# A linear-attention and mixture kernel on one core: the place of w_k's first half in the load queue, and a planner bias of 60000 or 20000

## The chip, the core and the metric

The kernel runs on one core of a Trainium2 chip. The metric is the device time of one execution in microseconds (us); less is better. The times shown are single executions of one program and their median.

## The reference

Inputs come as float64 or float32 arrays; the outputs are float32. Three stages follow one another:

- Linear attention on x (4 batches, 8 heads, 768 positions, 32 wide) with decay a and the projections B and C (16 wide), in chunks of 32 with a carried state: within a chunk `M = (C B^T) * exp(cum_i - cum_j)`, causal, and `y = M x`; across chunks `y += C state * exp(cum)`, and the state is decayed and updated by `B^T x`.
- A gated feed-forward on the 3072 tokens (256 wide): `xk` and `xr` mix each token with the one before it (`mu_k`, `mu_r`); `k = relu(xk w_k)` with w_k 256 x 1024, `v = k*k w_v`, `r = sigmoid(xr w_r)`, result `r * v`.
- A maxout layer: `h = max(x w1, x w2, x w3)` (768 wide), result `h w_out` (256 wide).

## The kernel before

**Tiles.** Tokens are worked on in six tiles of 512 (`t` = 0 to 5), features lie on the 128 partitions. For each tile the kernel computes attention, `gate` (mix, w_r, tanh), `ffn` (mix, w_k, square, w_v), `combine`, `maxout` and `final`. Every product is made of three fp32r products, high by high, high by low and low by high, so each operand exists as two tiles: a rounded copy (suffix h) and the remainder (suffix l). The remainder is made by `sub` (L421), which runs on VectorE (DVE) or GpSimd (POOL).

**Weights.** They arrive as float64 and are turned into the two fp32r tiles by `load_split` (L616): one load; one ACT instruction (L630); four DVE instructions on the bit patterns (L631, L633, L635, L637); one rounded copy (`copy`, L411, on ACT or DVE; the trace gives its line as L414 or L416); one `sub` (L422). For w_k's first half, the columns 0 to 511, this is done in two pieces of 128 rows, called w_k0 and w_k1 here (loop L659 to L661); each is 512 KB. The feed-forward of tile 0 needs both pieces in its first product group, w_k0 before w_k1 (L1006).

**The order of the work** is not written out: `Plan` (L76) collects every operation with its cost, its dependencies and a bias. `forward` (L138) simulates the five engines and SyncE's load queue (SP), and takes for each engine the ready operation with the smallest key minus bias. The key is minus the time from the operation to the end of the plan, in ns. It is re-estimated by `backward` in up to 60 rounds, and the round with the shortest modelled span is issued. A bias of 20000 thus lets an operation go ahead of work that is due up to 20 us sooner.

```
heapq.heappush(ready[e], (key[i] - ops[i][4] + (spare if len(costs) > 1 and e == "DVE" else 0.0), i))   # L191
plan.bias = AHEAD[1]                                                             # L656
..., 1, FF // 2, [b_wk[c][0]], FIRST[4] - 1.5e5 * c, place=spots[c])             # L661
```

The first loads are put in order by large values of FIRST that are added to the bias of the load alone (`dma`, L425). Before the change they stand as follows: a_l (`la`, 112 KB) 1.04e6, the mus 1.035e6 (2 KB), C padded with zeros (`cw`, 512 KB), B (`bt`, 256 KB) and w_k0 all 1.01e6, `bl` (256 KB) 1.005e6, w_r (512 KB) 1.003e6, x (`xt`, 512 KB) 1.0e6, C (`ct`, 256 KB) 0.98e6, w_k1 (512 KB) 0.86e6. All are issued from SP (L427). The loads of w_k's second half and of tile 1 depend on the operation at L848 (`ce`) (`after=k`, L663).

**The front of the kernel.** `attention(0)` (L793) spreads the decays (`spread_first`, L694: PE L703 and L704, ACT L708 into `lt`), forms the scores C B^T from bt and cw in two parts (`cb`, L860), multiplies them by the decays on DVE (L872, eight instructions), sums the values (L895), adds the carried part (L885) and copies the result to `xb` (L933). Then `mix` (L958) makes the inputs of `gate(None, 0)` (products L986) and of `ffn(None, 0)` (products L1011). Biases of the operations: attention(0) and w_r's preparation 20000, the tail of attention(0) 30000 less, gate 80000, w_k0 and w_k1 and the mix of ffn(0) 60000 (AHEAD). Until the first product of a gate the plan fills gaps of PE with dummy products (L1169, issued in L324 to L326). After that it does not.

Of the kernel before, what the change touches and what calls it, by code (L numbers as in the profile page):

```python
# [75 lines left out]
class Plan:  # L76
# [14 lines left out]
    FIRST = 1500.0  # L91
# [17 lines left out]
    def op(self, eng, cost, fn, r=(), w=(), after=(), issue=475.0, unless=None, hold=None, burst=0, lock=False):  # L109
        deps = set(after)  # L110
        for b in r:
            deps.update(b.writers)
        for b in w:
            deps.update(b.readers)
            deps.update(b.writers)
        i = len(self.ops)
        costs = eng if isinstance(eng, dict) else {eng: cost}
        self.ops.append((costs, fn, sorted(deps), issue, self.bias, unless, hold or {}, burst, lock))
        for b in w:
            b.writers = [i]  # L120
            b.readers = []
        for b in r:
            b.readers.append(i)
        return i
# [212 lines left out]
SPREAD = 2  # L337
LATE = 0
EARLY1 = -20000.0
AHEAD = (60000.0, 60000.0)  # L340
FIRST = (9.85e5, 9.8e5, 9.9e5, 9.83e5, 9.5e5, 9.95e5, 9.6e5)


# [1 line left out]
def kernel(  # L345
# [24 lines left out]
    FF = w_k.shape[1]  # L370
# [54 lines left out]
    def dma(cost, out_, in_, r=(), w=(), first=0.0, **k):  # L425
        plan.bias += first
        i = op("SP", 0.8 * cost, lambda: Q.dma_start(ap(out_), in_), r=r, w=w, **k)  # L427
        plan.bias -= first
        return i
# [15 lines left out]
    b_wk = [[Buf(), Buf()] for _ in range(KC)]  # L445
# [170 lines left out]
    def load_split(src, hi, lo, k, n, bufs, early=0.0, small=False, after=(), place=None):  # L616
        m = k * n
        if place:
            (sv, ss), (wv, ws) = place
        elif small:  # L620
            s, (wv, ws) = outr.next(), word2.next(m)
            sv, ss = s.ap[:, :2 * m], [s]
        else:
            (sv, ss), (wv, ws) = stage.next(2 * m), word.next(m)
        raw = sv.bitcast(U32).rearrange("p (k n s) -> p k n s", k=k, s=2)
        high, low = raw[:, :, :, 1], raw[:, :, :, 0]
        lf = wv.rearrange("p (k n) -> p k n", k=k)
        lu = lf.bitcast(U32)
        first = dma(m * 3.65, raw.rearrange("p k n s -> p k (n s)"), src.bitcast(U32), w=ss, first=early, after=after)
        op("ACT", act(m), lambda: A.activation(lf, high.bitcast(F32), AF.Abs), r=ss, w=ws)  # L630
        op("DVE", 68 + 0.521 * m, lambda: V.tensor_scalar(  # L631
            out=lf, in0=lf, scalar1=F64_LO, scalar2=F64_HI, op0=ALU.max, op1=ALU.min), w=ws, lock=True)
        op("DVE", 68 + 0.521 * m, lambda: V.tensor_scalar(  # L633
            out=lu, in0=lu, scalar1=5, scalar2=2, op0=ALU.logical_shift_left, op1=ALU.logical_shift_right), w=ws, lock=True)
        op("DVE", tt(m), lambda: V.scalar_tensor_tensor(  # L635
            out=lu, in0=high, scalar=0xC0000000, in1=lu, op0=ALU.bitwise_and, op1=ALU.bitwise_or), r=ss, w=ws, lock=True)
        op("DVE", tt(m), lambda: V.scalar_tensor_tensor(  # L637
            out=lu, in0=low, scalar=29, in1=lu, op0=ALU.logical_shift_right, op1=ALU.bitwise_or), r=ss, w=ws, lock=True)
        copy(hi, lf, m, ws, bufs)
        sub(lo, lf, hi, m, ws + bufs, bufs)  # L640
        return first
# [3 lines left out]
    def weights_front():  # L645
        plan.bias = BIAS[2]
        dma(100, mu.rearrange("p i c -> p (i c)"), mus, w=[b_mu], first=FIRST[5])
        op("DVE", 100, lambda: V.tensor_scalar(
            out=om, in0=mu, scalar1=-1.0, scalar2=1.0, op0=ALU.mult, op1=ALU.add), r=[b_mu], w=[b_om])
        fs = [slice(0, FF // 2), slice(FF // 2, FF)]  # L650
        wide, narrow = [Buf(), Buf()], [Buf(), Buf()]
        b_pre.extend(wide[:1] + narrow[:1])
        plan.bias = BIAS[1]
        load_split(w_r.rearrange("p (k n) -> p k n", k=KC), wr_t[0], wr_t[1], KC, CH, [b_wr], FIRST[3],
                   place=(stage.next(2 * TW), word.next(TW)))
        plan.bias = AHEAD[1]  # L656
        spots = [(stage.next(2 * TW), word.next(TW)), ((wo_f[0][:, :2 * TW], wide[:1]), word.next(TW)),
                 (stage.next(4 * TW), (wo_f[1][:, :2 * TW], narrow[:1]))]
        for c in range(KC):  # L659
            load_split(w_k[c * P:(c + 1) * P, None, fs[0]], wk_t[0][:, c:c + 1, fs[0]], wk_t[1][:, c:c + 1, fs[0]],  # L660
                       1, FF // 2, [b_wk[c][0]], FIRST[4] - 1.5e5 * c, place=spots[c])  # L661
        plan.bias = 0.0
        k = [begun['loads']]  # L663
        load_split(w_k[:, fs[1]].rearrange("(c p) n -> p c n", p=P), wk_t[0][:, :, fs[1]], wk_t[1][:, :, fs[1]],
                       KC, FF // 2, [b_wk[c][1] for c in range(KC)], FIRST[4] - 4e5, place=spots[2], after=k)
        inputs(1, (FIRST[4] - 4.2e5, FIRST[4] - 4.3e5), after=k)
        dma(935, bt.rearrange("p u i -> p (u i)"), b_t[1], w=[b_bt], first=FIRST[4] - 4.4e5, after=k)
        dma(1870, cw.rearrange("p u i -> p (u i)"), c_w[1], w=[b_cw], first=FIRST[4] - 4.5e5, after=k)
        dma(935, ct.rearrange("p u i -> p (u i)"), c_t[1], w=[b_ct], first=FIRST[4] - 2e5)
        for f in range(FC // 4):  # L670
            load_split(w_v[f].rearrange("p (k n) -> p k n", k=4), wv_t[0][:, 4 * f:4 * f + 4], wv_t[1][:, 4 * f:4 * f + 4], 4, CH, [b_wv[f]])
# [89 lines left out]
    def inputs(t, early=(0.0, 0.0), after=()):  # L761
        dma(935, bl.rearrange("p g n -> p (g n)"), b_l[t], w=[b_bl], first=early[0], after=after)
        dma(1870, xts[t % 2].rearrange("p g d -> p (g d)"), x_l[t], w=[b_xt[t % 2]], first=early[1], after=after)
        op({"DVE": tt(512), "POOL": pool(512)}, 0, lambda e: (V if e == "DVE" else G).tensor_mul(
            bd, bl, dfj[:, t * NG:(t + 1) * NG, None].to_broadcast([P, NG, N])), r=[b_bl, b_df], w=[b_bd], lock=True)
# [192 lines left out]
    def mix(i, dst, bufs, half, t):  # L958
        hv, cols, bs, n = tokens(half)
        xb, b_xb = xbs[t % 2], b_xbs[t % 2]  # L960
        for c in range(KC):
            tm = tmp.next()
            tv = tm.ap[:, :n].rearrange("p (b s) -> p b s", s=P)
            op({"DVE": 129 + 0.521 * n, "ACT": 93 + act(n)}, 0, lambda e, tv=tv, c=c: (
                V.tensor_scalar_mul(tv, xb[:, c, bs, 1:], mu[:, i, c:c + 1]) if e == "DVE" else
                A.activation(tv, xb[:, c, bs, 1:], AF.Copy, scale=mu[:, i, c:c + 1])),
               r=b_xb[bs] + [b_mu], w=[tm], lock=True)
            op("DVE", 61 + tt(n), lambda tv=tv, c=c: V.scalar_tensor_tensor(  # L968
                out=tv, in0=xb[:, c, bs, :P], scalar=om[:, i, c:c + 1], in1=tv, op0=ALU.mult, op1=ALU.add),
               r=b_xb[bs] + [b_om], w=[tm], lock=True)  # L970
            split(tm.ap[:, :n], tm, [d[:, cols] for d in dst[c]], [[bufs[c][s][h] for h in hv] for s in range(2)], n)
# [23 lines left out]
    def ffn(half, t):  # L995
        hv, cols, bs, n = tokens(half)
        xkt, b_xkt = xk_hl[t % 2], b_xk[t % 2]
        plan.bias += AHEAD[0] * (t == 0)
        mix(0, xkt, b_xkt, half, t)
        plan.bias -= AHEAD[0] * (t == 0)  # L1000

# [125 lines left out]
    plan.switch = begun['spread'], begun['carried']  # L1127
    plan.bias = 0.0
    weights_front()
    sums()  # L1130
    weights_back()
# [93 lines left out]
```

## Time and profile before

| | before |
|---|---|
| median of three runs | 407.53 us (407.53 to 408.23) |
| the profiled execution | 408.05 us |
| its span in the profile | 406.3 us |
| PE busy | 396.3 us, 98% of the span |
| DVE busy | 257.9 us, 63% |
| ACT busy | 216.1 us, 53% |
| POOL busy | 55.0 us, 14% |
| granted TensorE clock, mean | 0.998 |
| moved by DMA | 31.55 MB |

The span runs from the first to the last instruction of the profile; the execution's own time is 1.75 us longer. PE is TensorE's matmuls, PEld its weight loads, SPq the load queue of SyncE. A busy share over the whole span is a mean over stages with different limits: DVE has 63% of the span but is nearly full in its first third. In a row of the timeline the numbers are start and duration in us, then engine, line, operation, output and inputs; the bracket gives the idle time of that engine before it and what ended it.

### The profile page before, as it was taken

Reading aid. Unit: us, or ns where it says so; the run is one execution under the profiler, and the core shown is the slowest. Engines: PE = TensorE matmul, PEld = TensorE weight load, DVE = VectorE, ACT = ScalarE, POOL = GpSimd, SP = SyncE. Lnnn points to the kernel's source line nnn. Section 1 sums busy time; section 2 is a strip of 40 time slices with the busy share of each in tenths; the row PEclk is TensorE's granted clock in tenths of the full one; section 3 lists DMA queues with packets and bytes.
Section 4 is the critical chain, followed back from the end, with each engine's and each line's share of the span. In section 5 each row is a group of like instructions: output and inputs, shape, how many; then the busy total and the mean of one; then the engine's idle time right before and its main releaser. Section 6 shows DMA issues by size and latency. Waiting matters only on the chain.

```text
span 406.3 us, 8667 instructions
## 1 busy us (share of the span) xinstructions
PE 396.3 (98%) x3684; PEld 318.0 (78%) x3684; DVE 257.9 (63%) x417; ACT 216.1 (53%) x379; POOL 55.0 (14%) x60
## 2 busy tenths in 40 slices
PE   8789999999999999999999999999999999999996
PEld 5557877788877888888888888888787888888885
DVE  5898999999998945573735473755373315430632
ACT  6489878954767743355743255753246733321321
POOL 5121000000004100421400231320022200010010
PEclk9999999999999999999999999999999999999999
DMA  7596559541335200206100002300000000001001
GB/s 251 187 369 193 180 139 259 164 141 33 129 112 152 73 26 0 71 38 177 31 27 0 28 2 66 66 26 0 2 2 27 0 26 2 0 0 54 0 2 52
DMA packets 12879, 31.55 MB, mean 78 GB/s; under 512 B 1768, under 2 KB 4136, under 8 KB 12072
## 3 DMA queue, kind: packets, MB, share of 16 engines
q1 hardware_dynamic: 12840, 30.99, 24.7%
q8 instruction: 29, 0.48, 0.5%
q14 instruction: 10, 0.08, 0.1%
HBM read 27.64 MB, written 3.34 MB: 76 GB/s over the span
## 4 chain that ended last, share of the span: by engine, by line
PE 80%; DVE 13%; issue 2%; DMA 2%; ACT 2%; SPq 0%; DVEq 0%; ACTq 0%
PE pa L689 32%; PE pa L1032 14%; PE pa L1011 13%; PE pa L1108 9%; PE pa L986 3%; PE pb L1108 2%; DVE L L872 2%; DVE tmp L1070 1%; PE pb L895 1%; DMA h<-in_w_k_dram 1%; PE pb L860 1%; DVE k2l L422 1%; DMA outs<-in_w_out_dram 1%; DVE tmp L968 1%; DVE h L637 1%
## 5 line engine op out<-in xcount | busy, mean ns | idle before, releaser
L1070 DVE TENSOR_TENSOR tmp<-tmp,pa 128x512 f32<-128x512 f32 x72 | 49.0, 684 | 55.3 <-PE pa L689 54.5
L422 DVE TENSOR_TENSOR k2l<-tmp,k2h 128x512 fp32r<-128x512 f32 x53 | 39.9, 764 | 40.9 <-ACT tmp L1020 34.0
L414 ACT ACTIVATE hr<-tmp 128x512 fp32r<-128x512 f32 x35 | 22.1, 632 | 69.3 <-DVE tmp L1070 69.1
L1032 PE MATMUL pa<-k2h,wvh 128*128 128x512 f32 x96 | 38.2, 398 | 0.0
L1032 PE MATMUL pa<-k2h,wvl 128*128 128x512 f32 x96 | 38.0, 395 | 0.0
L1032 PE MATMUL pa<-k2l,wvh 128*128 128x512 f32 x96 | 37.8, 393 | 0.0
L1108 PE MATMUL pa<-hr,worh 128*128 128x512 f32 x120 | 37.4, 393 | 0.0
L1017 ACT ACTIVATE tmp<-pa 128x512 f32<-128x512 f32 x48 | 28.3, 590 | 10.3 <-PE pa L1011 8.6
L1068 ACT ACTIVATE tmp<-pa 128x512 f32<-128x512 f32 x36 | 21.5, 598 | 21.8 <-PE pa L689 20.2
L1018 ACT ACTIVATE k2h<-tmp 128x512 fp32r<-128x512 f32 x48 | 30.2, 631 | 2.6 <-PE pa L1032 1.0
L422 DVE TENSOR_TENSOR hr<-tmp,hr 128x512 fp32r<-128x512 f32 x28 | 19.5, 700 | 14.8 <-ACT hr L414 14.7
L1108 PEld LDWEIGHTS pa<-hr,worh 128*128 128x128 f32 x120 | 22.3, 188 | 5.3 <-ACT th L991 0.7
L422 POOL TENSOR_TENSOR hr<-tmp,hr 128x512 fp32r<-128x512 f32 x8 | 10.3, 1292 | 110.8 <-ACT hr L414 110.8
L1020 ACT ACTIVATE tmp<-tmp 128x512 f32<-128x512 f32 x37 | 23.2, 630 | 0.8
L1108 PE MATMUL pa<-hr,worl 128*128 128x512 f32 x60 | 23.4, 389 | 0.0
L1032 PEld LDWEIGHTS pa<-k2h,wvh 128*128 128x128 f32 x96 | 18.0, 188 | 4.4 <-ACT k2h L414 0.2
L1032 PEld LDWEIGHTS pa<-k2h,wvl 128*128 128x128 f32 x96 | 18.0, 188 | 4.4
L1032 PEld LDWEIGHTS pa<-k2l,wvh 128*128 128x128 f32 x96 | 18.0, 188 | 4.1
L790 POOL TENSOR_TENSOR sbd<-sbd,um 128x256 f32<-128x256 f32 x2 | 3.1, 1548 | 117.8 <-DVE sbd L788 117.8
L1079 ACT ACTIVATE outs<-pa 128x512 f32<-128x512 f32 x9 | 5.4, 600 | 25.5 <-PE pa L1108 25.5
L968 DVE SCALAR_TENSOR_TENSOR tmp<-xb,bits,tmp 128x512 f32<-128x512 f32 x24 | 17.2, 745 | 0.3
L872 DVE TENSOR_TENSOR L<-pb,L 128x512 f32<-128x512 f32 (+1 forms) x28 | 15.7, 603 | 1.6 <-PE pb L860 0.8
(273 smaller groups left out, 977.4 us busy)
## 6 DMA issues: line engine op xcount, KB each, us to landing
h<-in_w_dram SPq DMA_DIRECT2D x6, 768.0 KB, 5.0
L<-crd SPq DMA_DIRECT2D x8, 512.0 KB, 6.9
cw<-in_c_w_dram SPq DMA_DIRECT2D x6, 512.0 KB, 4.5
xt<-in_x_l_dram SPq DMA_DIRECT2D x6, 512.0 KB, 7.8
out_dram<-outs SPq DMA_DIRECT2D x10, 256.0 KB, 2.0
h<-in_w_v_dram SPq DMA_DIRECT2D x2, 1024.0 KB, 7.6
bt<-in_b_t_dram SPq DMA_DIRECT2D x6, 256.0 KB, 4.7
bl<-in_b_l_dram SPq DMA_DIRECT2D x6, 256.0 KB, 6.5
```

What stands on the lines that cost most here:

```text
L414: A.activation(ap(out_), ap(in_), AF.Copy)
L422: op({"DVE": tt(n), "POOL": pool(n, narrow)}, 0, lambda e: (V if e == "DVE" else G).tensor_sub(ap(out_), ap(x0), ap(x1)), r=r, w=w, after= ...
L689: T.matmul(pt, l, r_, start=(i == 0), stop=(i == last))
L872: op("DVE", tt(2 * step * HP), lambda q=q, b=b, lq=lq: V.tensor_mul(lq, W[q].ap[:, b * P:(b + step) * P].rearrange("p (b r i) -> p r b i", ...
L1011: T.matmul(p.ap[:, :n], l, r_, start=(c == 0 and i == 0), stop=(c == KC - 1 and i == 2))
L1017: op("ACT", 51 + 0.833 * n, lambda: A.activation(sq, p.ap[:, :n], AF.Relu), r=[p], w=[tm])
L1018: op("ACT", act(n), lambda: A.activation(hi, sq, AF.Square), r=[tm], w=[kb])
L1020: A.activation(sq, sq, AF.Square) if e == "ACT" else
L1032: T.matmul(pv[c2].ap[:, :n], l, r_, start=(f == 0 and i == 0), stop=(f == FC - 1 and i == 2))
L1068: op("ACT", 51 + 0.833 * TW, lambda p=p, tm=tm: A.activation(tm.ap, p.ap, AF.Copy), r=[p], w=[tm])
L1070: op("DVE", tt(TW), lambda p=p, tm=tm: V.tensor_tensor(out=tm.ap, in0=tm.ap, in1=p.ap, op=ALU.max), r=[p], w=[tm])
L1108: T.matmul(p.ap, l, r_, start=(g == 0 and i == 0), stop=(g == GC - 1 and i == 2))
```

## The change

AHEAD goes from 60000 to 20000 in both places, and the load of the first half of w_k has AHEAD subtracted. The bias of w_k0's load becomes 20000 + 9.5e5 - 20000 = 0.95e6 instead of 1.01e6, and of w_k1's 0.80e6 instead of 0.86e6. The preparation of w_k0 and w_k1 and the mix of ffn(0) have a bias of 20000 instead of 60000. No operation is added or removed; the plan is made anew from these values.

```diff
@@ -337,7 +337,7 @@
 SPREAD = 2
 LATE = 0
 EARLY1 = -20000.0
-AHEAD = (60000.0, 60000.0)
+AHEAD = (20000.0, 20000.0)
 FIRST = (9.85e5, 9.8e5, 9.9e5, 9.83e5, 9.5e5, 9.95e5, 9.6e5)
@@ -658,7 +658,7 @@
         for c in range(KC):
             load_split(w_k[c * P:(c + 1) * P, None, fs[0]], wk_t[0][:, c:c + 1, fs[0]], wk_t[1][:, c:c + 1, fs[0]],
-                       1, FF // 2, [b_wk[c][0]], FIRST[4] - 1.5e5 * c, place=spots[c])
+                       1, FF // 2, [b_wk[c][0]], FIRST[4] - AHEAD[1] - 1.5e5 * c, place=spots[c])
         plan.bias = 0.0
```

## Rows read from the trace of the kernel before

**Rows 1.** The page, part 1: busy time, share of the span, instructions.

```profile
PE 396.3 (98%) x3684; PEld 318.0 (78%) x3684; DVE 257.9 (63%) x417; ACT 216.1 (53%) x379; POOL 55.0 (14%) x60
```

**Rows 2.** Busy time by stretch: length, PE, PEld, DVE, ACT, POOL, granted clock, DMA share, GB/s.

```profile
26.15:402.90 376.75, 375.31 (x3184) 303.71 (x3182) 237.58 (x377) 198.16 (x347) 45.12 (x32) 1.00 0.22 64
37.73:120.80 83.07, 82.16 (x966) 65.61 (x952) 82.78 (x139) 62.36 (x112) 0.00 (x0) 1.00 0.51 151
```

**Rows 3.** Who PE waited for from 26.15 to 402.9: total, times, longest.

```profile
PE pa L1011 <- ACT tmp L1017: 0.8, 1, 0.8
PE pa L1011 <- DVE outs L1081: 0.4, 1, 0.4
```

**Rows 4.** Timeline of PE: a stall, the first gate product, the first ffn product.

```profile
23.99 0.46 PE L727 MATMUL pb<-tri,la 64*64 64x64 f32 x16 [1.54 <-issue]
...
26.15 0.58 PE L986 MATMUL pa<-k2h,wrh 128*128 128x512 f32 x1
...
29.12 0.39 PE L1011 MATMUL pa<-xk00h,wkh 128*128 128x512 f32 x1
```

**Rows 5.** Timeline of SP's load queue: issue time and duration, loaded tile and source.

```profile
1.70 0.43 SPq L427 DMA_DIRECT2D h<-in_w_k_dram  x1
2.17 0.43 SPq L427 DMA_DIRECT2D cw<-in_c_w_dram  x1
2.65 0.43 SPq L427 DMA_DIRECT2D bt<-in_b_t_dram  x1
...
3.64 0.48 SPq L427 DMA_DIRECT2D h<-in_w_r_dram  x1
...
5.33 0.50 SPq L427 DMA_DIRECT2D woh<-in_w_k_dram  x1
```

**Rows 6.** Busy time by stretch up to three landings; the last column is GB/s.

```profile
0.00:6.18 6.18, 5.17 (x110) 4.30 (x111) 3.18 (x9) 4.21 (x7) 5.08 (x23) 1.00 0.58 152
0.00:9.13 9.13, 7.57 (x116) 5.19 (x117) 5.62 (x15) 5.96 (x10) 5.38 (x24) 1.00 0.73 232
0.00:10.92 10.92, 9.36 (x151) 6.04 (x151) 6.72 (x16) 7.07 (x12) 6.44 (x25) 1.00 0.78 262
```

**Rows 7.** Timelines of ACT and PE: the first users of three loads, and the decays.

```profile
6.21 0.67 ACT L630 ACTIVATE h<-h 128x512 f32<-128x512 f32 x1 [0.34 <-DMA h<-in_w_k_dram]
...
7.53 0.60 ACT L708 ACTIVATE L<-pa 128x512 f32<-128x512 f32 x1 [0.17 <-PE pa L704]
...
9.13 0.70 PE L860 MATMUL pb<-cw,bt 32*64 32x128 f32 x32 [0.56 <-DMA bt<-in_b_t_dram]
...
10.92 0.67 ACT L630 ACTIVATE h<-h 128x512 f32<-128x512 f32 x1 [0.51 <-DMA h<-in_w_r_dram]
```

**Rows 8.** Timeline of DVE: w_k0's preparation, the scores, the last input of ffn(0).

```profile
6.91 0.43 DVE L631 TENSOR_SCALAR h<-h 128x512 f32<-128x512 f32 x1 [0.41 <-ACT h L630]
...
8.58 0.69 DVE L637 SCALAR_TENSOR_TENSOR h<-h,h 128x512 uint32<-128x512 uint32 x1
9.96 1.44 DVE L422 TENSOR_TENSOR wkl<-h,wkh 128x512 fp32r<-128x512 f32 x1 [0.70 <-ACT wkh L414]
11.32 0.41 DVE L872 TENSOR_TENSOR L<-pb,L 128x256 f32<-128x256 f32 x1
12.55 2.08 DVE L872 TENSOR_TENSOR L<-pb,L 128x256 f32<-128x256 f32 x6 [0.82 <-PE pb L860]
15.45 0.42 DVE L872 TENSOR_TENSOR L<-pb,L 128x256 f32<-128x256 f32 x1 [0.82 <-PE pb L895]
...
27.51 0.68 DVE L422 TENSOR_TENSOR wkl<-wd,wkh 128x512 fp32r<-128x512 f32 x1
28.11 0.68 DVE L422 TENSOR_TENSOR xk01l<-tmp,xk01h 128x512 fp32r<-128x512 f32 x1
```

**Rows 9.** Busy time in the stretch from w_k0's first DVE instruction to ffn(0)'s last input.

```profile
6.91:28.79 21.88, 17.68 (x402) 11.73 (x401) 19.09 (x35) 14.43 (x29) 4.48 (x4) 1.00 0.78 304
```

**Rows 10.** Timeline of POOL beside w_k0's remainder.

```profile
9.79 1.06 POOL L764 TENSOR_TENSOR bd<-bl,dfj 128x512 f32<-128x512 f32 x1 [3.23 <-DMA bl<-in_b_l_dram]
```

## The prediction

> **What bounds the kernel now.** I read the page's busy shares first, then the busy time by stretch, PE's waits, and the timelines of the front. PE is busy for 98% of the span [rows 1], so the question is where the rest lies and what stands ahead of the dense part. From 26.15 to 402.90 us PE is busy 375.31 of 376.75 us [rows 2], and the view of waits shows only two there, 0.8 and 0.4 us [rows 3]. The first gate product starts at 26.15 and the first product of the feed-forward of tile 0 at 29.12 [rows 4]. The end is therefore the start of the dense part, plus PE's work, plus 1.2 us of waits, plus a tail that the change does not touch.
>
> DVE looks idle by its mean, 63% [rows 1]. But from 37.73 to 120.80 us it is busy 82.78 of 83.07 us [rows 2], the one window where the feed-forward, the next attentions and all weight preparations run together. Both PE waits of the dense part lie in that window. So work cannot simply be pulled forward there: PE could start earlier, but what DVE owes it would not come earlier. Time is gained only if DVE loses less in its first 38 us, and it is lost if DVE loses more.
>
> **Step 1, the loads.** In the queue w_k0 goes out at 1.70, ahead of cw at 2.17 and bt at 2.65; w_r goes at 3.64 and w_k1 at 5.33 [rows 5]. By the new values w_k0 (0.95e6) stands behind ct (0.98e6), so it is issued ninth, at about 4.7. The number of loads and their bytes stay, and w_k1 keeps the last place. The others move up one place, about 0.5 us in issue and 512 KB in bytes.
>
> When do they land? Up to 6.18, 9.13 and 10.92 us the core had moved 152, 232 and 262 GB/s times those lengths, that is 0.94, 2.12 and 2.86 MB [rows 6]. At these times w_k0, bt and w_r had just been taken up by their users [rows 7]. In queue order the bytes up to and with them are 0.64, 1.43 and 2.21 MB, so a load was usable when 0.30 to 0.69 MB more than its share had moved. With the change bt's share is 0.90 MB; it is usable at 1.20 to 1.59 MB, and at 0.40 MB per us past 6.18 that is 6.8 to 7.8 us instead of 9.13. w_r comes at about 9.7 instead of 10.9. w_k0's share is 3.00 MB; it comes at about 12.8 instead of 6.2. All three are estimates from these rows.
>
> **Step 2, attention(0).** The scores' products (L860) take 0.70 us. Their DVE instructions (L872) also need the decays, the second of which ACT ends at 8.13 [rows 7]. Now DVE reaches L872 only at 11.32, because w_k0's remainder stands in front of it from 9.96 [rows 8]. With the change it can start at 7.5 to 8.6, and not before 8.1: I take 8.1 to 8.6. That is a lead of 2.7 to 3.2 us for attention(0), and it is the gain that the change offers.
>
> **Step 3, w_k0 on DVE.** What the lead costs is that w_k0's five DVE instructions no longer fill the time before the scores. They are two of 0.43, two of 0.69 and the remainder at 1.44 [rows 8], 3.7 us in all; with the remainder at the 0.68 of w_k1's [rows 8] it would be 2.9. Two ACT instructions move with them, the first of 0.67 [rows 7]. They now come after 12.8 us, among w_r, w_k1, the copy of xb and the mixes, all of which DVE must do before the first products. So I make DVE's account to the end of ffn(0)'s last mix input, xk01l, at 28.79 [rows 8]. Between 6.91 and 28.79 DVE is busy 19.09 us [rows 9], the same work in both kernels but for a cast of 0.2 that can go before the scores: 18.9. Of the other 2.79, it waits 0.70 for w_k0's rounded copy and twice 0.82 around the scores [rows 8]; 0.45 is left.
>
> With the change it starts at 8.1 to 8.6. The first 0.82 (the second scores wait for PE) stays, because w_r is not usable until 9.7 and then needs ACT first. The second 0.82 is filled by w_r's instructions or stays; the 0.45 stays. The end is 8.1 + 18.9 + 1.27 = 28.3 at best and 8.6 + 18.9 + 2.09 = 29.6 at worst, against 28.79: from 0.5 less to 0.8 more. I take the worse end, +0.8: w_r's preparation needs its ACT instruction of 0.67 behind its landing while ACT still owes two decays, so little of it is ready for the second gap.
>
> One row speaks for a smaller sum. w_k0's remainder took 1.44 instead of 0.68 us while POOL multiplied `bd` from 9.79 on [rows 8, 10]; with the change `bd` runs beside the scores. The Trainium skill ("SBUF — State Buffer", section "Who interferes with whom") says that a DVE instruction contends with GpSimd's reads only with two inputs in SBUF or in a two-port mode. The scores have one input in PSUM, so by that rule the 0.76 us would vanish and the account would stand at -1.3 to 0.0. That rule argues for the faster rival; no row shows a score instruction beside a POOL instruction of this size, and three of w_k0's instructions with two SBUF inputs may meet POOL later, so I keep the 0.76 in the sum.
>
> **Step 4, the rest of the plan.** With a bias of 20000 instead of 60000 the preparation of w_k0 and w_k1 and the mix of ffn(0) rank level with attention(0) and w_r, behind the gate's mix. The plan is also made anew, so every later tie can fall differently. This cost is bounded from one side: PE has 1.2 us of waits in 376.75 [rows 2, 3], so reordering can win at most that, while new waits have no such limit. For a price I take the smaller wait that the dense part has, 0.4 us; the larger one, 0.8, and PE's stall of 1.54 at 23.99 [rows 4] are bounds above. That stall is covered now, since the gate's inputs are not ready until 26.15. If the gate comes forward it is covered less.
>
> **Sum.** +0.8 (DVE's account) and +0.4 (one more small wait) make +1.2 us. On the profiled execution (408.05, of which 406.3 is the span) that is 409.25. That execution lies 0.52 above the median of 407.53, so against the median the same sum gives 408.7, the forecast. 0.2% of the median is 0.8 us, about what a measurement of this kernel can tell from no change.
>
> **The rivals.**
> - **Faster: the lead goes through.** The gate's inputs follow attention(0), and its mix has the highest bias (80000). If w_r is ready in time and DVE's account ends 0.5 early, or 1.3 early with the 0.76 saved, PE's dense part starts earlier by that much: 407.0 to 406.2. If w_k0 were wholly hidden, the lead of 2.7 would be the limit, 404.8. For it: bt is the scores' last releaser [rows 7], and a remainder that nobody needs before 29 us stands in front of them. Against it: DVE is full behind 37.73 [rows 2]. It decides if the first gate product comes before about 25.5 with ffn(0) following at once. Chance 0.28.
> - **Slower by more: w_k0 falls behind the gate.** With its bias lowered by 40000, w_k0's five DVE instructions may be placed after the gate's mix. PE then finishes the gate and waits for them: 2.9 to 3.7 us, of which attention(1)'s spread can cover part. That gives about 410.4, and up to 411.6 with a further 0.4. It decides if the first ffn product comes after about 31. Chance 0.17.
> - **No difference: the account is even.** DVE ends at 28.79 within 0.5 us and PE's waits stay: 406.9 to 408.2. PE uses xk01 only a few products after the first at 29.12, so a small delay is covered there. I add to this case the small chance that the change does not do what it says: the keys differ by the time at which work is due, a few ten thousand ns, and the distance to ct is only 30000, so w_k0 might still pass a load. Chance 0.25.
>
> **How the numbers follow.** The forecast itself, slower by 0.8 to 2 us (408.3 to 409.5), gets 0.30. It and the late w_k0 make 0.47 for slower, the even account 0.25 for the same, the lead 0.28 for faster. The predicted time is that of the forecast, 408.7. The range goes down to 405.9, which holds the faster rival but for its limit, and up to 411.6, which holds the late w_k0 with one wait more.
>
> **What would show it.** Right: in the load queue cw and bt first and w_k0 ninth; bt's wait at L860 ending before 8 us; L872 starting by 8.6; w_k0's ACT instruction at 12 to 13; xk01l ending at 28.8 to 29.7; PE's waits in the dense part above 1.2 us. Wrong: a first gate product before 25.5 with no new waits behind it (faster), or L872 still at 11. If DVE's account is even and yet PE's waits between 38 and 121 us grow by more than 2 us, the cause is the new plan and not w_k0, and step 3 carries nothing.

## The result, and the profile after

The changed kernel takes 414.64 us (median of four runs: 408.98, 414.60, 414.68, 414.81) against 407.53 for the kernel before in the same series. The ratio, which goes by all the runs and not by the two medians, is 1.0129, 95% interval 1.0093 to 1.0164. The prediction said slower by 1.2 us and gave a range up to 411.6; by the medians it was slower by 7.1. One run lies 5.6 us below the other three. Its mean granted clock was 0.999, theirs 0.991 to 0.996, and that gap is itself part of what has to be explained. The profiled execution took 414.81 us, with a span of 413.1.

SP's load queue after, issue time and duration (to be set beside [rows 5]):

```profile
1.71 0.42 SPq L427 DMA_DIRECT2D cw<-in_c_w_dram  x1
2.17 0.43 SPq L427 DMA_DIRECT2D bt<-in_b_t_dram  x1
...
3.13 0.43 SPq L427 DMA_DIRECT2D h<-in_w_r_dram  x1
...
4.57 0.43 SPq L427 DMA_DIRECT2D h<-in_w_k_dram  x1
5.05 0.53 SPq L427 DMA_DIRECT2D woh<-in_w_k_dram  x1
```

The queue is as forecast: cw and bt lead, w_k0 is ninth. The front then does gain. DVE's timeline after, first scores and last input of ffn(0), against [rows 8]:

```profile
10.68 0.74 DVE L872 TENSOR_TENSOR L<-pb,L 128x256 f32<-128x256 f32 x2
...
27.78 0.68 DVE L422 TENSOR_TENSOR xk01l<-tmp,xk01h 128x512 fp32r<-128x512 f32 x1
```

The scores start 0.6 us sooner than before, xk01l ends at 28.46 instead of 28.79. PE's timeline after shows what that gave and where it went, against [rows 4]:

```profile
21.83 0.52 PE L986 MATMUL pa<-k2h,wrh 128*128 128x512 f32 x1
...
27.95 0.50 PE L1011 MATMUL pa<-xk00h,wkh 128*128 128x512 f32 x1
...
43.77 0.62 PE L1011 MATMUL pa<-xk00h,wkh 128*128 128x512 f32 x1 [4.26 <-ACT tmp L1017]
44.19 0.63 PE L1011 MATMUL pa<-xk00l,wkh 128*128 128x512 f32 x1
...
59.62 0.70 PE L895 MATMUL pb<-L,xt 64*32 64x64 f32 x46 [2.63 <-issue]
```

The first gate product comes at 21.83, 4.3 us sooner than 26.15, and the first product of ffn(0) at 27.95 instead of 29.12. Then PE stands 4.26 us at an L1011, the products behind it take 0.63 us instead of 0.39, and at 56.99 PE stops in the middle of the 128 products of L895 with no releaser in the profile (the bracket of the last row). The time by stretch says the same: the first two rows and the last cut the span at the first gate product and 4 us before the end, the second and third are to be set beside [rows 2], and the fourth is the stretch of slow products behind the wait. The column behind the engines is the granted clock: it is 0.53 there, the lower of TensorE's two levels (1.2 GHz of 2.4).

```profile
0.00:21.83 21.83, 19.34 (x496) 13.41 (x496) 15.26 (x37) 13.71 (x26) 6.27 (x25) 1.00 0.65 218
21.83:409.10 387.27, 379.09 (x3183) 306.03 (x3182) 242.62 (x381) 202.65 (x353) 50.21 (x33) 0.99 0.23 68
37.73:120.80 83.07, 75.89 (x852) 60.60 (x851) 75.58 (x123) 56.92 (x99) 0.00 (x0) 0.96 0.47 136
43.77:47.17 3.40, 3.40 (x8) 2.65 (x9) 3.40 (x6) 1.38 (x2) 0.00 (x0) 0.53 0.03 11
409.10:413.10 4.00, 0.50 (x3) 0.08 (x1) 0.45 (x2) 0.38 (x1) 0.00 (x0) 0.94 0.39 131
```

From 37.73 to 120.80, where PE was busy 82.16 of 83.07 us before, it is busy 75.89. DVE, full before (82.78), is busy 75.58 there, 7.2 us less.

Such rows make an account of the span: PE's idle time (length less busy) in three stretches, the dummy products (L1169 and L1171), and the rest, which is PE's real work. The rest grows where the clock falls. A second execution of the changed kernel (the first experiment) and two later kernels are set beside it.

| us | span | idle to the first gate product | idle from there to 4 us before the end | idle in the last 4 | dummies | rest |
|---|---|---|---|---|---|---|
| before | 406.3 | 5.20 | 1.36 | 3.49 | 6.28 | 389.97 |
| after | 413.1 | 2.49 | 8.18 | 3.50 | 4.81 | 394.12 |
| the changed kernel, first experiment below | 409.8 | 2.83 | 6.88 | 3.48 | 4.82 | 391.79 |
| eleventh kernel below | 408.0 | 2.38 | 3.26 | 3.50 | 8.86 | 390.00 |
| twelfth kernel below | 413.1 | 8.36 | 0.82 | 3.54 | 6.73 | 393.65 |

After against before: 2.7 less idle and 1.5 less dummy work, which is the 4.2 us by which the gate came sooner; 6.8 more idle behind it; and 4.2 more in the rest. Of the last, two stretches of eight products at a spacing of 0.43 instead of 0.23 us make 3.1. The sum is the 6.8 us of the two spans. The second execution has neither slow stretch and is 3.5 us longer than before: 5.5 more idle behind the gate and 1.8 more in the rest, whose cause no run isolates, less 3.8 ahead of the gate. So the new waits are there in both executions, and about half of the loss comes on top in some of them.

Who PE waited for, in the second of the stretches (total, times, longest), against [rows 3]:

```profile
PE pa L1011 <- ACT tmp L1017: 4.5, 2, 4.3
PE pb L895 <- issue: 2.6, 1, 2.6
PE pa L1011 <- DVE wkl L422: 0.4, 1, 0.4
PE pa L986 <- DVE k2l L422: 0.4, 1, 0.4
```

**The first loss** is followed back on ACT, whose timeline shows why the relu (L1017) that PE needs was late:

```profile
41.17 1.12 ACT L630 ACTIVATE wd<-h 128x1024 f32<-128x1024 f32 x1 [2.44 <-DMA h<-in_w_v_dram]
42.19 1.05 ACT L414 ACTIVATE wvh<-h 128x1024 fp32r<-128x1024 f32 x1
43.13 0.59 ACT L1017 ACTIVATE tmp<-pa 128x512 f32<-128x512 f32 x1
```

ACT works in the order of the plan. It stood at the preparation of w_v's second half until that load had landed, and behind it stood the relu, which needed no load at all. In the kernel before, ACT reached this L630 after the load was there, and did not wait (no bracket):

```profile
42.21 1.15 ACT L630 ACTIVATE wd<-h 128x1024 f32<-128x1024 f32 x1
```

The views of DMA issues from 28 to 48 us (size, and us from issue to landing) give the load itself, before and then after:

```profile
h<-in_w_v_dram SPq DMA_DIRECT2D x1, 1024.0 KB, 4.9
```

```profile
h<-in_w_v_dram SPq DMA_DIRECT2D x1, 1024.0 KB, 7.4
cw<-in_c_w_dram SPq DMA_DIRECT2D x1, 512.0 KB, 6.5
bt<-in_b_t_dram SPq DMA_DIRECT2D x1, 256.0 KB, 6.7
```

It was issued 2.0 us sooner (33.75 instead of 35.74) and landed 0.5 us later (41.15 instead of 40.6). The loads of cw and bt follow it at the same distance in both (2.2 and 2.6 us); what stands closer is the load ahead of it, `ec` from `ced` (256 KB), issued at 31.25 before, 4.5 us ahead, and at 31.89 after, 1.9 us ahead. The Trainium skill ("DMA: Bandwidth & Descriptors", section "Anatomy of one DMA — SWDGE (gpsimd) path") fits one transfer on GpSimd's path, which is not the path of this load from SyncE, as 2.0 us plus its bytes over 436 GB/s. As an estimate that is 4.4 us for a megabyte; the row of before is near it, the row of after is not.

**The second loss** is the 2.63 us of L895. What the traffic suggests is that PE waits for its own code. The views of DMA queues after, from 52.60 to 57.00 us (first row) and then from 57.00 to 58.00 (packets, MB, share), show a packet of instructions only in the second; the view does not tell for which engine:

```profile
q1 hardware_dynamic: 260, 0.77, 69.9%
...
q8 instruction: 1, 0.02, 5.9%
```

SP's queue after shows what had been issued ahead of it:

```profile
52.57 0.38 SPq L427 DMA_DIRECT2D h<-in_w_dram  x1
```

The 768 KB load was issued at 52.57, 0.77 MB moved until 57, then the one code packet (from 57.40 to 58.35), and PE went on at 59.62. Whether this explains the stall, the experiments had to say.

### The profile page after: what moved, and what is told of

Read it like the earlier page. It is cut to its first block, busy times and chain, and to the rows that moved or that the text cites. A ratio compares the mean times of both kernels' runs of the same rounds, so it can differ in the third digit from the quotient of the medians.

```text
span 413.1 us, 8657 instructions
## 1 busy us (share of the span) xinstructions
PE 398.9 (97%) x3678; PEld 319.5 (77%) x3678; DVE 258.3 (63%) x418; ACT 216.7 (52%) x379; POOL 56.5 (14%) x58
## 4 chain that ended last, share of the span: by engine, by line
PE 79%; DVE 10%; DMA 7%; issue 2%; ACT 2%; SPq 1%; DVEq 0%; ACTq 0%
PE pa L689 30%; PE pa L1032 17%; PE pa L1011 13%; PE pa L1108 9%; PE pa L986 3%; PE pb L1108 2%; DMA ced<-h 2%; DMA h<-in_w_v_dram 2%; DVE tmp L1070 2%; PE pb L895 2%; DMA h<-in_w_r_dram 1%; DMA h<-in_w_k_dram 1%; DVE L L872 1%; PE pb L885 1%; PE pb L860 1%
## 5 line engine op out<-in xcount | busy, mean ns | idle before, releaser
L414 ACT ACTIVATE hr<-tmp 128x512 fp32r<-128x512 f32 x36 | 22.7, 632 | 71.5 <-DVE tmp L1070 71.3
L1032 PE MATMUL pa<-k2h,wvh 128*128 128x512 f32 x96 | 39.1, 407 | 0.0
L1032 PE MATMUL pa<-k2l,wvh 128*128 128x512 f32 x96 | 38.7, 403 | 0.0
L1017 ACT ACTIVATE tmp<-pa 128x512 f32<-128x512 f32 x48 | 28.5, 594 | 11.0 <-PE pa L1011 8.5
L790 POOL TENSOR_TENSOR sbd<-sbd,um 128x256 f32<-128x256 f32 x2 | 6.8, 3420 | 116.9 <-DVE sbd L788 116.9
L968 DVE SCALAR_TENSOR_TENSOR tmp<-xb,bits,tmp 128x512 f32<-128x512 f32 x24 | 18.1, 777 | 0.3
L872 DVE TENSOR_TENSOR L<-pb,L 128x512 f32<-128x512 f32 (+1 forms) x28 | 16.0, 605 | 1.0 <-PE pb L860 0.9
```

The source lines that it names most:

```text
L414: A.activation(ap(out_), ap(in_), AF.Copy)
L872: op("DVE", tt(2 * step * HP), lambda q=q, b=b, lq=lq: V.tensor_mul(lq, W[q].ap[:, b * P:(b + step) * P].rearrange("p (b r i) -> p r b i", ...
L1017: op("ACT", 51 + 0.833 * n, lambda: A.activation(sq, p.ap[:, :n], AF.Relu), r=[p], w=[tm])
L1032: T.matmul(pv[c2].ap[:, :n], l, r_, start=(f == 0 and i == 0), stop=(f == FC - 1 and i == 2))
```

## The experiments

Three theories were set against each other. **A:** ACT, and DVE behind it, stand in their fixed order at loads that land later than their place in the order needs, and PE starves. **B:** the price is what the prediction's step 3 priced, w_k0's late preparation on DVE. **C:** PE's code is queued behind a load, and the clock falls after the long waits. The second to eighth, tenth and eleventh kernels edit the changed kernel, the ninth and twelfth the kernel before. Of each edit the lines that matter are shown; `split_ld`, `split_in`, `split_hi` and `relu` are lists of operations (loads, their L630, the rounded copies, L1017) in the order in which they are made, and a new `start` moves one operation in its queue, nothing else. The kernel before took 406.6 to 411.4 us in the series of the first eight, so small ratios are not told apart there; kernels of one series are compared with the same runs of before. It has executions with a low mean clock too: over the three series, 20 of its 66 runs lie below 0.998, against 7 of the 10 of the changed kernel.

**1. The changed kernel once more.** No edit.

> The changed kernel itself, unchanged. Theory A (an ACT instruction that takes up the second half of w_v, L630 wd, stands in ACT's order ahead of the rounded copy of w_v's first half and of the relu that frees PE's bank; the load lands 7.4 us after its issue, so PE idles 4.26 us at 39.5 to 43.8, then runs at the lower clock, and meets a code stall of 2.6 us): times near 409 and near 414.7 again, the lower ones with a mean granted clock of 0.999. Theory B (w_k0's preparation on DVE after 12.8 us costs the time, as forecast): one level, within 1 us.

Measured: 413.06 us, ratio 1.0102 (1.0057 to 1.0147), runs from 410.31 to 415.18. Its profiled execution, 411.62 us, holds neither the code stall nor slow products, though PE waited 2.67 us:

```profile
44.95 0.50 PE L1011 MATMUL pa<-xk00h,wkh 128*128 128x512 f32 x1 [2.67 <-ACT tmp L1017]
45.29 0.40 PE L1011 MATMUL pa<-xk00l,wkh 128*128 128x512 f32 x1
```

So the L1011 wait belongs to the kernel, while the code stall and the slow clock come in some executions and not in others. The size of the wait follows ACT's: here ACT stood 0.86 us at w_v's second half (L630 at 42.34) instead of 2.44, but 3.38 us at w_k's second half (at 26.17), and PE's first feed-forward product waited 1.32 us for a tanh behind that. Over all ten runs of the changed kernel, those with a clock of 0.999 took 408.98 to 411.62, the other seven (0.991 to 0.996) 411.48 to 415.18.

**2. The late load alone.** The old biases, w_k0's load still ninth.

```diff
-AHEAD = (20000.0, 20000.0)
+AHEAD = (60000.0, 60000.0)
```

> Only the place of the load changes: w_k0 ninth in the queue as in the changed kernel, the biases 60000 as before. Theory A: the late w_k0 itself costs little, the time depends on what the new plan puts in front of a late load: between 407 and 410 unless the trace shows a PE wait over 2 us between 35 and 65 us. Theory B: the late w_k0 costs on DVE whatever the biases: 409 to 411, with ffn(0)'s last mix input later than 28.8.

Measured: 412.86 us, ratio 1.0119 (1.0066 to 1.0173). The gate starts at 27.93, ffn(0) at 34.00, later than in either kernel. Its chain of waits has theory A's mark at another load:

```profile
21.95 10.27 DMA h<-in_w_v_dram
...
32.32 1.13 ACT h L630
33.46 0.50 ACT th L991
...
34.00 3.02 PE pa L1011 x12
```

ACT stood 4.29 us at the first half of w_v, with the gate's tanh behind it, and PE's first feed-forward product waited for that tanh. The load was not slower than in the kernel before (10.36 us there), it was issued 2.5 us later. Both theories expected 411 or less and were missed; theory B's sign, xk01l later than 28.8, is not there: it ended at 27.87. From 37.73 to 120.80 PE is busy 82.98 of 83.07 us, so this kernel loses its time mostly ahead of that stretch and not in it.

**3. The lower biases alone.** w_k0's load third, ahead of cw.

```diff
-                       1, FF // 2, [b_wk[c][0]], FIRST[4] - AHEAD[1] - 1.5e5 * c, place=spots[c])
+                       1, FF // 2, [b_wk[c][0]], FIRST[4] + 40000.0 - 1.5e5 * c, place=spots[c])
```

> Only the biases change: 20000 instead of 60000, but w_k0's load keeps its place ahead of cw and bt. Theory A: the front is like before (first gate product near 26 us), 406.5 to 409 unless a load stands in ACT's way. Theory B: 407.5, as before, since w_k0 is early.

Measured: 411.28 us, ratio 1.0051 (1.0021 to 1.0082). DVE prepares w_k0 early again (the remainder ends at 11.29, the scores start at 11.21), so theory B has nothing left to charge here, and the kernel is still slower. Its profile has a code stall of 1.73 us at L895. The new plan alone costs something, without w_k0 being late; both theories expected 409 or less. Either half of the change makes the kernel slower by itself, and the halves do not add up: each is a plan of its own.

**4. One ACT instruction later.** w_v's second half is prepared behind the relu that PE waited for.

```diff
-    plan.arrange()
+    plan.arrange(); plan.start[plan.split_in[5]] = plan.start[plan.relu[4]] + 0.5
```

> The changed kernel with one ACT instruction (L630 wd, second half of w_v) moved behind the two that stood after it (the rounded copy of w_v's first half and one relu). Nothing else moves on any engine. Theory A: PE's wait of 4.26 us falls to 2.5 or less, the products behind it keep the full clock, and the time falls to 408 to 411.5. Theory B: no change, 414 to 415.

Measured: 411.96 us, ratio 1.0070 (1.0035 to 1.0105). The profiled execution, 407.9 of span, has a wait of 1.88 us at L1011 instead of 4.26 and no code stall. By its median alone, just above the 408 to 411.5 expected, it is not told apart from the changed kernel. Its views of DMA queues from 52.4 to 53 us (first row) and from 53 to 54 hold a control for theory C:

```profile
q8 instruction: 1, 0.02, 11.0%
...
q1 hardware_dynamic: 17, 0.05, 70.0%
```

The same 768 KB load was issued at 52.50 here, but PE had come further by then: its products of L773, which stand shortly ahead of L895, started at 50.53, 2.0 us ahead of the load. The code packet moved (from 52.42) ahead of the load's bytes, and there is no stall. In the changed kernel the two stood at 52.47 and 52.57.

**5. Two ACT instructions later.** As the fourth, and w_k's second half is prepared behind the copy it stood in front of.

```diff
+    plan.start[plan.split_in[3]] = plan.start[plan.split_hi[2]] + 0.5
```

> The changed kernel with two ACT instructions moved back in ACT's order: the one of w_v's second half as in the run before, and L630 wol (second half of w_k, which waited 0.6 to 3.4 us for its load) behind the rounded copies of xk00, xk01 and w_k1. Theory A (ACT, in its fixed order, waits for loads that land later than the plan assumes, and PE starves behind it): no ACT wait for a DMA before 45 us, ffn(0) starts before 28 us, and the lowest time comes to 405 to 408. Theory B (w_k0 on DVE): no gain over the run with one instruction moved, lowest 409.

Measured: 409.45 us, ratio 1.0053 (1.0012 to 1.0094), runs from 408.22 to 413.68; the runs with a clock of 0.999 or 1.0 took 408.22 to 409.51, so the lowest just missed the 405 to 408 expected. The profiled one was the longest (413.68), and it shows the two marks without any long wait of ACT for a load ahead of 45 us:

```profile
PE pb L895 <- issue: 2.6, 1, 2.6
PE pa L1011 <- ACT tmp L1017: 2.2, 2, 1.9
```

The wait of L1011 stays at 1.87 us though ACT waits for no load there: this part is the plan's order. The relu stands behind the rounded copy of w_v's first half, which waited 1.07 us for DVE (L414 at 40.31). PE's wait less ACT's wait for the load is nearly the same wherever ACT waits: 1.82 (after, 4.26 less 2.44), 1.81 (first experiment, 2.67 less 0.86) and 1.84 us (tenth, 2.71 less 0.87). It is 1.87 to 1.89 in the fourth, fifth, sixth and eighth, where ACT does not wait for it. So what ACT waits for the load, PE pays in full. The load was issued at 51.03, 0.4 us after L773 at 50.62, and the code packet came behind it.

**6. A load to the front.** w_k's second half goes out directly behind w_k1.

```diff
+    plan.start[plan.split_ld[3]] = plan.start[plan.split_ld[2]] + 0.5
```

> The changed kernel with one load issued sooner: w_k's second half (1 MB) directly behind w_k1 at about 5.6 us, not behind ce at 17.3. All engines keep their order. Theory A: the load is there before ACT asks for it, the loads behind it (tile 1, w_v) come 2 us or more sooner, the PE waits at 37 to 44 us shrink below 2 us, and the time falls below 409 with no run over 412. Theory B: 409 to 415 as the changed kernel, since w_k0's place is the same.

Measured: 411.30 us, ratio 1.0055 (1.0019 to 1.0092). The hope of under 409 was missed: the first gate product slipped to 22.84, the wait of 1.88 at L1011 and a code stall of 2.20 at L895 were both there.

**7. PE kept busy in the wait.** Ten dummy products ahead of the L1011 that waited.

```diff
-            if where[i]:
+            if [self.filler(False) for _ in range(10 * (i == self.gap))] or where[i]:
```

> The changed kernel with 10 dummy products (L1169) on PE in front of the first-half product that waited 4.26 us (L1011 at 43.77). The wait itself is not touched. If the clock drop behind long PE waits is a cause of its own, runs near 414.7 go away, the highest stays under 413, and no product of 0.63 us follows this place. If it is not, the spread stays 409 to 415.

Measured: 411.35 us, ratio 1.0062 (1.0025 to 1.0099). The profiled execution shows a clock of 1.00 there, 0.63 us of wait behind 2.33 us of dummies, and no code stall; but a run of 414.68 still came. The L1011 wait is therefore not the only source of the long executions, and the expectation of none over 413 was missed.

**8. The fourth and the sixth together.**

```diff
+    plan.start[plan.split_ld[3]] = plan.start[plan.split_ld[2]] + 0.5; plan.start[plan.split_in[5]] = plan.start[plan.relu[4]] + 0.5
```

> The load of w_k's second half in front and the ACT instruction of w_v's second half moved back, together. Theory A: the lead of 4 us at the gate now lasts longer; PE waits between 28 and 62 us sum to under 2 us and the time is 403.5 to 407, below the kernel before. Theory B: 408 or more.

Measured: 409.74 us, ratio 1.0037 (1.0008 to 1.0066). The gate starts at 24.62; L1011 still waits for tmp three times, 3.0 us in all. The 403.5 to 407 expected by theory A was missed: the gate's lead was mostly gone.

**9. The same load to the front in the kernel before.**

```diff
+    plan.arrange(); plan.start[plan.split_ld[3]] = plan.start[plan.split_ld[2]] + 0.5
```

> The kernel before with one change in the order of SyncE's queue: the load of w_k's second half is issued directly behind w_k1's, instead of behind the operation at L848. Everything else keeps the plan of before. Theory A (ACT, in its fixed order, stands waiting for weight loads that land later than the plan assumes, and PE starves): in before no ACT instruction waits long for a load ahead of 45 us, so there is little to win; the queue is one load longer in the front, no user comes later than before by more than 0.5 us: 407.2 to 408.8, PE's waits from 26 to 403 us below 2 us. Theory B (the price lies in w_k0's late preparation on DVE): no change, since w_k0 stays early: within 0.3% of before. Theory C (the code request behind the later load, and the clock): no change unless that load's issue moves; within 0.3% of before.

Measured: 407.94 us, ratio 0.9995 (0.9973 to 1.0017). In the kernel before, ACT never waited for this load, and nothing is won by bringing it sooner.

**10. The borders of PE's code blocks moved.** 48 dummy products at PE's start in place of 104.

```diff
-                for _ in range(0 if idle else self.EARLY):
-                    self.narrow()
+                for m in range(0 if idle else 48):
+                    self.narrow() if m < 40 else self.filler(False)
```

> The changed kernel with 48 dummy products (40 narrow, 8 wide) at PE's start in place of 104 narrow ones, so that the same later product lies 56 matmuls earlier in PE's code and the borders of the code blocks fall on other products. Theory C (PE's code block is asked for behind the 768 KB load that DVE releases, and PE stalls with no releaser in the profile): no wait for issue of over 1 us at L895 near 57 us, unless the border falls on another point just behind a load; the runs above 412.5 vanish; 409 to 411. Theory A: the wait of L1011 for tmp at 40 to 44 us remains, with the late landing of w_v's second half ahead of it; without a further cause 410 to 412. Theory B: no effect on the time, 411 to 414.

Measured: 412.18 us, ratio 1.0111 (1.0094 to 1.0128), four runs from 411.73 to 412.57. PE's waits from 18 to 403 us:

```profile
PE pa L1011 <- ACT tmp L1017: 3.8, 2, 2.7
PE pa L689 <- issue: 0.8, 1, 0.8
PE pa L1011 <- ACT outs L1079: 0.5, 1, 0.5
```

Nothing else of the plan was changed. In this profile the wait for code is gone from L895; 0.8 us stands at another line. The load was issued 0.11 us behind the start of L773, as in the changed kernel, but the code packet had moved at 51.86, ahead of both. The four runs lie within 0.9 us, the ten of the changed kernel within 6.2. The level of 409 to 411 was missed, and the clock was low in two stretches: in the first 20 us (0.92) and from 40 to 60 us (0.91), where the L1011 wait is still there. The fewer products at the start do not explain the first by themselves: the eleventh kernel has the same ones and kept 1.00.

```profile
0.00:20.00 20.00, 17.17 (x360) 10.79 (x360) 11.86 (x30) 9.87 (x18) 6.11 (x25) 0.92 0.54 182
40.00:60.00 20.00, 17.29 (x308) 13.55 (x308) 18.39 (x28) 13.21 (x22) 0.00 (x0) 0.91 0.51 166
```

**11. The fifth, the seventh and the tenth together.**

> The changed kernel with three edits together: the two ACT instructions that waited for late weight loads stand behind the instructions PE was waiting for (as in the fifth kernel), ten dummy products before the L1011 that waited (as in the seventh), and the code borders moved (as in the tenth). Theory A with C: no ACT wait for a load of over 1 us ahead of 45 us, no wait for issue of over 1 us at L895, no products of 0.63 us between 42 and 65 us; lowest run about 407, median 408 to 409, no run above 411.5. Theory B: w_k0's late preparation is still there, so 411 to 413. If the median stays at 409.5 or above with all three marks gone from the profile, part of the loss is in the new plan's order itself and is named by none of them.

Measured: 409.81 us, ratio 1.0062 (1.0042 to 1.0081), runs from 409.43 to 411.10. PE's waits from the first gate product to 4 us before the end:

```profile
PE pa L1032 <- ACT xb L933: 1.3, 1, 1.3
PE pa L1011 <- ACT outs L1079: 0.6, 1, 0.6
PE pa L1011 <- DVE wkl L422: 0.5, 1, 0.5
PE pa L1011 <- ACT tmp L1017: 0.3, 1, 0.3
```

All three marks are gone from the profile, the clock is 1.00, and the table's rest is 390.00, that of before. Still it is not as fast as before, and the median is above the 409.5 from which the expectation blamed the new order itself. The account says why: the gate starts 3.1 us sooner (2.8 less idle), but behind it there are 1.9 us more of idle and 2.6 more of dummies, of which 2.33 are the ten that fill the wait at L1011. PE's early start is spent in the dense part on having nothing to do. DVE is busy 82.02 of the 83.07 us from 37.73 to 120.80, nearly as full as before, so it had little room to give PE its work sooner. DVE, at work 72.60 us of the first 80 in the kernel before, is at work 70.84 here; the first product of `final` comes at 121.34 instead of 119.83, later by 1.5 us, about that deficit.

**12. The late load under the old plan.** The kernel before, all engines in their old order, only w_k0's load moved to the ninth place.

```diff
+    plan.arrange(); plan.start[plan.split_ld[1]] = plan.start[plan.split_ld[2]] - 0.5
```

> The kernel before, its plan kept, with only w_k0's load moved to the ninth place of the queue (directly ahead of w_k1's), so the order of all engines stays that of before. ACT then stands at w_k0's instruction (L630) until about 12.8 us instead of 6.2, with the decays (L708) behind it, and DVE with it. Theory A (the price is a fixed order of an engine that does not match when loads land): first gate product 4 to 6 us later than 26.15, 411.5 to 413.5, all of it ahead of 30 us, and PE's waits behind 38 us as small as before's. Theory B (the price of w_k0's late preparation on DVE): about the same lateness here, since this is the strongest form of it; it would be told apart from A by DVE's busy time from 0 to 40 us, which by B is as low as in the changed kernel's stretch from 40 to 80. Theory C: the lateness is there from the start and stays constant to the end; no stall of PE's code at L895 unless the second w load is issued ahead of it.

Measured: 415.17 us, ratio 1.0188 (1.0171 to 1.0204). The first rows of ACT's and PE's timelines that matter:

```profile
12.70 0.66 ACT L630 ACTIVATE h<-h 128x512 f32<-128x512 f32 x1 [6.77 <-DMA h<-in_w_k_dram]
13.26 1.07 ACT L708 ACTIVATE L<-pa 128x512 f32<-128x512 f32 x2
```

```profile
17.53 1.16 PE L860 MATMUL pb<-cw,bt 32*64 32x128 f32 x32 [7.05 <-DVE L L872]
...
33.33 0.58 PE L986 MATMUL pa<-k2h,wrh 128*128 128x512 f32 x1
```

ACT stands 6.77 us at w_k0 with the decays behind it. DVE stands 6.82 us at w_k0's first instruction, works through all five, and comes to the scores at 17.05 instead of 11.32. The gate starts 7.2 us late. The lateness goes through unchanged (first product of `final` 7.1 us late) and behind it PE idles 0.82 us. The size was 7.2 instead of the 4 to 6 expected; the granted clock of 0.79 over the first 40 us may be part of it, which no run tests. The sign that was to tell theory B apart is there too, with DVE busy only 24.43 of the first 40 us, so this run does not separate the two by that number. What its rows show is theory A's path: w_k0's instructions are the same work as before, and one load behind its place in the engines' order is paid in full.

## Why the prediction was right or wrong

**The direction was right, but by luck: the larger of the two terms that made it, DVE's account, came out with the other sign. The prediction failed in step 4.**

- **Step 1, the loads: right.** Order and ninth place as forecast. w_r's ACT instruction ran at 9.17 (forecast 9.7). w_k0's ran at 13.40, where the load had landed at 13.12, and in the twelfth kernel at 12.70 (forecast 12.8): working out landings from bytes moved held within about half a microsecond. L860 no longer waited for bt.
- **Step 2, the lead: wrong in its path, larger in its end.** L872 came at 10.68 and not at 8.1 to 8.6. bt was there, but PE made the scores' products (L860) only at 9.01 to 9.70, behind products that spread the decays, where it had made them at 9.13 before. And two instructions for w_r (L631, L633 at 9.87 and 10.33) now stood in front of L872; ahead of them DVE was idle 1.39 us until ACT had taken up w_r. Even so the gate came 4.3 us sooner, more than the 2.7 to 3.2 granted to the scores: the whole chain to the gate was re-ordered, with w_k0's remainder and most of w_k1's preparation moved behind the gate's mix.
- **Step 3, DVE's account: the premise did not carry.** xk01l ended at 28.46, 0.3 sooner, where +0.8 was taken. The late w_k0 cost nothing by 28.5 us, xk01l is not late in the second kernel either (27.87), and the third kernel, where w_k0 is early, is slower all the same. As a cost on DVE ahead of ffn(0), theory B falls. The remainder of w_k0 took 0.68 us at 26.57; in the third kernel, with `bd` on POOL at 9.69 beside it, it took 1.35. The rule weighed there (the Trainium skill, "SBUF — State Buffer", section "Who interferes with whom") is consistent with both. The case it was weighed for did not come up: `bd` ran on DVE at 7.65 and not beside the scores on POOL. The account was not what decided.
- **Step 4, the rest of the plan: the failed step.** It was put at +0.4 us. The text said that reordering could win at most 1.2 us while new waits had no such limit, and then priced them by the smallest wait that the trace of before happened to show. In the profiled execution the term measured 6.8 us of new idle behind the gate. Another 4.2 us came in the rest, most of it slow products, for which the prediction had no term at all. Against these 11 stand the 4.2 us by which the gate came sooner. In the second execution it was 5.5 us of idle and 1.8 in the rest. The text named the right test, PE's waits between 38 and 121 growing by more than 2 us with DVE's account even, and by that test "the cause is the new plan and not w_k0". They grew by 6.3 us, and by 3.0 in the second execution. One reading was wrong on the way: of the two PE waits of before, only the 0.8 lies in the stretch where DVE is full; the 0.4 is at 125.89.
- **The rivals.** "The lead goes through" had its point of decision, a gate before 25.5 with ffn(0) following; the gate met it, ffn(0) did not follow at once (27.95), and the chain broke 16 us later. The argument against it, that DVE is full behind 37.73, fits the eleventh kernel: with every mark removed, a gate 3 us sooner was worth nothing. "w_k0 falls behind the gate" is what happened in part (its remainder ran at 26.57), but without the price: the first ffn product did not come after 31.

What the runs show of the 7.1 us, then. **Shown:** ACT's stand at w_v's second half, 0.9 to 2.4 us from one execution to the next, which PE pays in full (the differences under the fifth experiment), and 1.8 us of wait at the same place that is the plan's order. **Shown, but not as a cause of its own:** some 2 us that stay with every mark removed (eleventh, 1.0062); the new order, the late w_k0 and the ten dummies are all in that kernel, and no run parts them. **Worked out, not isolated:** the slow products, 3.1 us in the profiled execution. **Supported, not forced:** the code stall of up to 2.6 us at L895. It is absent from the tenth kernel's one profile, but also from the second of the changed kernel. The distance from the start of L773 to the load's issue sorts most profiles: in four with the stall it is 0.10 (after), 0.41 (fifth), 0.44 (sixth) and -3.0 us (third), in seven without it 1.65 to 2.19 us (before and kernels 1, 4, 7, 8, 9, 11). The tenth (0.11) and the second (-2.9) have no stall, and the code packet's own time fits all of them. It moved 4.9, 4.7, 4.3 and 2.5 us behind the start of L773 in the four with the stall, and PE went on 1.2 to 1.6 us after the packet had passed. In six of the seven without it, it moved 1.7 to 1.9 us behind that start. In the tenth and eleventh, whose code borders lie elsewhere, it moved 0.7 and 0.4 us ahead of it; in the second at 55.27, when that load was nearly over and PE came to L895 only at 57.13. No kernel moved that load alone. What decides whether the clock falls after a wait stays open.

## What to carry to other kernels

A statically ordered kernel absorbs a late transfer only where the waiting instruction has nothing urgent behind it: before moving a load, list for each engine what stands behind its first user, because those are what will be late. And when a change makes a scheduler plan anew, price the new plan by the slack of the loads that it will issue at other times, and not by the smallest wait of the old trace: the old trace shows how the old order goes, and nothing of what a new one can lose. An early start of the busiest engine was worth nothing here, where its suppliers were not earlier too: account for the supplier up to the end of its full stretch.

## What was not expected of the hardware

- A load of one megabyte took 4.9 us where the load ahead of it had been issued 4.5 us sooner, 7.4 us where it was 1.9 us, and 6.5 us in the eleventh kernel, where it was 1.6 us. The first half of w_v took 10.36 us in the kernel before and 10.27 in the second, where only its later issue made ACT wait. What each of them waited for was not isolated.
- Code seems to wait behind data: a stall of 1.73 to 2.64 us in PE, in the middle of a run of equal products, where the packet of instructions came after most of a 768 KB load. The Trainium skill ("Runtime: NRT & Kernel Launch", section "Instruction fetch mechanics") calls the cost of crossing a block mostly hidden. In four profiles here it was not, if the stall is that cost, and there the measurement decides.
- The granted clock after a wait is not told by the wait's length: after 1.87 us (fifth kernel) products of 0.63 us followed at once, after 1.88 us (sixth) they followed 1.3 us later, and after 1.88 (fourth) and 2.67 us (first) none did. Two such stretches of eight products cost 3.1 us in the changed kernel's profile, as much as a stall.
